# Dense layers of a long-convolution kernel: 25 tiles instead of 26, 22 of them 512 columns wide

## Chip, cores and metric

The kernel runs on one core of one Trainium2 chip. The metric is the device time of one execution in microseconds, as the median of several runs. Profiles are of one execution each; their times count from the first instruction of the span.

## What is computed

```
x, v: (1, 12480, 128)    pos_emb: (12480, 64)    w1: (64, 64)    w2: (64, 128)
h = relu(pos_emb @ w1) @ w2 * exp(-0.01 * pos)          # the filter, 12480 taps
y = irfft(rfft(x * v, 2S) * rfft(h, 2S))[:S]            # causal convolution along the sequence
a = x * y
a = relu(a @ moe_w_in) ** 2 @ moe_w_out                 # dense layer pair 1, width 2048
out = elu(a @ moe2_w_in) @ moe2_w_out                   # dense layer pair 2, width 2048
```

All of it is in fp32 in the reference; S = 12480, d_model = 128.

## The kernel before

The convolution is a two-factor Fourier transform of length 181 x 127 (`N1`, `N2`). A position is n1 * 127 + 63 + s * p: a row (p, s) holds the up to 99 positions (`R`) that share their distance p from the middle of a block of 127 and the side s. There are 127 rows, 98 or 99 positions each. Phase 1 folds and transforms the inputs over n1, phase 2 transforms over n2, multiplies by the filter's spectrum, transforms back over k2 and stores the result as `Zd` in DRAM. The last transform back, over k1, is done in phase 3, tile by tile, just ahead of the dense layers.

Columns here are positions. `SIZES` cuts the 127 rows into tiles: 4 rows, 24 times 5 rows, 3 rows. [...]

Phase 3 works on 26 tiles x 8 steps, written out as one sequence of steps `s`; the program order on each engine is the order in which this Python emits it (no scheduler moves it). For a tile and a step u, 256 of the 2048 hidden units are done:

- `mm1` multiplies the tile by a block of input weights, `mm2` adds the product with the output weights into the tile's y bank. Both use `mm6`: numbers and weights are split in a high and a low part, and six one-pass matmuls (type fp32r, 128 x 128 weights, the tile's columns as the moving operand) make up one product of two blocks (hi x hi, hi x lo, lo x hi). Each has a weight load of its own. A step has 24 such matmuls: 12 for `mm1` and `mm2` of the first layer pair (l = 0), 12 for those of the second (l = 1), which runs `LEAD` = 11 steps behind on an earlier tile.
- ScalarE and VectorE make the activations (L860, L864, L871 for pair 1; L795, L796, L852, L878 and a copy at L148 for pair 2). The low parts are subtractions at L145 (`sub`): on GpSimd for pair 1, on VectorE for pair 2 (`lo_of`).
- `fin` copies y out: to the second pair's input, or as `ys` to the output in DRAM.
- For the last tile (`t == NT - 1`) the second pair's `mm2` uses whole weights `wl` and plain fp32 matmuls (L751), two instead of six, each recorded as two.

Ahead of its first step a tile is loaded and prepared. `load(t)` issues eight transfers on SP's queue: five pieces of `Zd` into z, then the tile's transform tables ta and tb and its x. z, x, ta and tb have two buffers each, so a load waits for the preparation two tiles before it. It is emitted at step 0 of tile t - 2, tile 1's before the loop. `prep(t)` is a generator of which two pieces are emitted per step, from step 0 of tile t - 1 on (tile 1's from step 3 of tile 0): three operations on VectorE (L697), the transform back `ymm2` on TensorE (L619, L623, into a borrowed PSUM bank), the product with x on VectorE (L705), the rounding copy xh on ScalarE (L148) and the low part xl on VectorE (L145). xh and xl are what `mm1` reads. Tile 0's are made at the end of phase 2.

PSUM is full in phase 3: one double bank `h`, two double banks `h2`, two y banks. One bank holds 512 fp32 columns.

The output's columns, x and the tables stand in the order of the tiles' rows (`_perm`, `cols`).

Of the kernel before, what the change touches and what calls it, by code (L numbers as in the profile page):

```python
# [10 lines left out]
F32 = mybir.dt.float32  # L11
F32R = mybir.dt.float32r
U32 = mybir.dt.uint32
AF = mybir.ActivationFunctionType
ALU = mybir.AluOpType
# [4 lines left out]
S = 12480  # L20
D = 128
# [3 lines left out]
N2 = 127  # L25
CEN = N2 // 2
# [4 lines left out]
KA = K1 - 64  # L31
R = 99
SPLIT = S - (R - 1) * N2
SIZES = (4,) + 24 * (5,) + (3,)
KTAIL = K1 - 64
TBB = 6
WF = 5
# [19 lines left out]
def _tiles():  # L57
    seq = [(p, s) for p in range(CEN + 1) for s in (1, -1) if p or s == 1]
    out = []
    b = 0  # L60
    for g in SIZES:
        part = seq[b:b + g]
        right = [p for p, s in part if s == 1]
        left = [p for p, s in part if s == -1]
        if not out:
            part = [(p, 1) for p in right] + [(p, -1) for p in left]
        out.append((right, left, [R if s < 0 and CEN - p < SPLIT else R - 1 for p, s in part], part))
        b += g
    assert b == len(seq)
    return out  # L70


def tables():
    n1 = np.arange(R)
    k1 = np.arange(K1)
    k2 = np.arange(N2)
    pe, po = np.arange(CEN + 1), np.arange(1, CEN + 1)
    t = {}
    th = _angle(n1[:, None] * k1[None, :], N1)
    t["t1"] = np.stack([np.cos(th), -np.sin(th), -np.cos(th)], axis=2).reshape(R, 3 * K1)  # L80
    tf = np.zeros((2 * NP, N2, N2))
    k = k1[:, None, None] + N1 * k2[None, None, :]
    tf[:K1, :CEN + 1] = np.cos(_angle(pe[None, :, None] * k, L))
    tf[:K1, 0] = 0.5
    tf[:K1, CEN + 1:] = np.sin(_angle(po[None, :, None] * k, L))
    t["tf"] = np.zeros((NP, 128, 2 * N2))
    t["tf"][:, :N2] = tf.reshape(NP, 2, N2, N2).swapaxes(1, 2).reshape(NP, N2, 2 * N2)
    th = _angle(k2[:, None] * pe[None, :], N2)
    g = np.zeros((128, 128))
    g[:N2, 0] = 1.0  # L90
    g[:N2, 1:N2:2] = np.cos(th)[:, 1:]
    g[:N2, 2:N2:2] = np.sin(th)[:, 1:]
    t["g"] = g
    tl = _tiles()
    order = [s * p for p, s in tl[0][3]]
    at = _perm() - CEN
    c = np.where(k1 == 0, 1.0, 2.0)[:, None] / L
    th = _angle(k1[:, None] * at[None, :], L)
    re, im = c * np.cos(th), -c * np.sin(th)
    n = sum(tl[0][2])  # L100
    t["t3"] = np.stack([re[:, :n].reshape(K1, SIZES[0], -1), im[:, :n].reshape(K1, SIZES[0], -1)], axis=2)
    t["t3"] = t["t3"].reshape(K1, -1)
    t["ta"] = np.concatenate([re, im[:KA]])
    side = np.concatenate([np.full(nr, s) for _, _, nrs, rows in tl for (p, s), nr in zip(rows, nrs)])
    t["tb"] = np.concatenate([np.where(side == s, im[KA:], 0.0) for s in (1, -1)])
    sg = np.ones((128, 3))
    sg[:K1, 0] = sg[K1:, 1] = sg[K1 - KA:, 2] = -1.0
    t["sg"] = sg
    th = _angle((k[2 * PD:, 0, :, None, None] *
                 (np.array(order)[:, None] + N2 * n1[None, :R - 1])[None, None]), L).reshape(KD, N2, -1)  # L110
    t["t4"] = np.zeros((128, 2 * th[:, 0].size))
    t["t4"][:N2] = (2.0 / L * np.stack([np.cos(th), -np.sin(th)], axis=1)).transpose(2, 0, 1, 3).reshape(N2, -1)
    pos = _taps().astype(np.float32)
    ok = (pos >= 0) & (pos < S)
    win = np.where(ok, np.exp(np.float32(-0.01) * np.where(ok, pos, np.float32(0.0))), 0.0)
    win = win.transpose(2, 0, 1).reshape(R, 8, 2, 4, 2).transpose(0, 1, 2, 4, 3).reshape(R, 128)
    t["wz"] = np.concatenate([win, np.zeros((128 - R, 128))])
    return {k: np.ascontiguousarray(a, dtype=np.float32) for k, a in t.items()}
# [8 lines left out]
    return np.concatenate([a, np.zeros((1, a.shape[1]), a.dtype)])[np.where((at >= 0) & (at < S), at, S)]  # L127


def _perm():  # L130
    return np.concatenate([np.arange(nr) * N2 + CEN + s * p for _, _, nrs, rows in _tiles()
                           for (p, s), nr in zip(rows, nrs)])


class Build:
# [14 lines left out]
    def setup(self):  # L150
        nc = self.nc
        const = self.const = self.pool("const")
        self.dram = self.pool("dram", 1, DRAM)
        self.zero = const.tile([128, 128], F32, name="zero")
        nc.vector.memset(self.zero, 0.0)
        self.ebias = const.tile([128, 3], F32, name="ebias")
        self.sg = const.tile([128, 3], F32, name="sg")
        nc.vector.memset(self.ebias[:, 0:1], 1151.0)
        nc.vector.memset(self.ebias[:, 1:2], 255.0 * 8388608.0)
        self.Z = self.dram.tile([K1, 128, 2 * D], F32, name="Zd")  # L160
        self.wp = self.pool("wp")
        self.tiles = _tiles()
        self.st = {}

    def big(self, i, dt=F32):
# [439 lines left out]
    def cols(self, a, t):  # L605
        c = sum(sum(nrs) for _, _, nrs, _ in self.tiles[:t])
        return a[:, c:c + sum(self.tiles[t][2])]

    def ymm(self, ps, v, t3):
        for i in range(SIZES[0]):  # L610
            o = ps[i // 2][:, (R - 1) * (i % 2):(R - 1) * (i % 2 + 1)]
            for ri in range(2):
                self.nc.tensor.matmul(o, lhsT=v[:, i, ri, :], rhs=t3[:, i, ri], start=False, stop=(i % 2 == 1 and ri == 1))
# [24 lines left out]
    def phase3(self):  # L638
        nc, a = self.nc, self.a
        ctx0 = self.ctx  # L640
        with ExitStack() as self.ctx:
            gh = self.pool("gh3", 3)
            gp = self.pool("gp3", 2)
            xp = self.pool("xp3", 2)
            wk = self.pool("wk3", 1)
# [3 lines left out]
            psl = self.pool("psl", 2, PSUM)  # L649
            psy = self.pool("psy", 1, PSUM)  # L650
            tl = self.tiles
            NT = len(tl)
            xin = {}
            yps = {}
            lds = {}

            def width(t):
                n = sum(tl[t][2])
                return n, n + n % 2

            def load(t):
# [27 lines left out]
            def prep(t):  # L689
                right, left, nrs, rows = tl[t]  # L690
                n, ne = width(t)
                z, x, ta, tb, v, p0 = lds.pop(t)
                ka = K1 + KA
                for i, (side, k) in enumerate(((right, ka), (left, ka), (None, 128))):
                    q = slice(side[0] - p0, side[-1] - p0 + 1) if side else slice(0, v.shape[2])
                    zi = z[:k, i // 2, q]
                    nc.vector.scalar_tensor_tensor(out=v[:k, i, q], in0=zi[:, :, 1], scalar=self.sg[:k, i:i + 1],  # L697
                                                   in1=zi[:, :, 0], op0=ALU.mult, op1=ALU.add)
                    yield
                yield  # L700
                ps = aux()[:, 0]
                post.append(lambda: self.ymm2(ps, v, ta, tb, rows, nrs, p0))
                yield
                at = row(wk, "at")
                nc.vector.tensor_tensor(out=at[:, :n], in0=ps[:, :n], in1=x, op=ALU.mult)  # L705
                yield
                xh, xl = row(xp, "xh", F32R), row(xp, "xl", F32R)
                if ne > n:
                    nc.vector.tensor_copy(xh[:, n:ne], self.zero[:, 0:1])
                    nc.vector.tensor_copy(xl[:, n:ne], self.zero[:, 0:1])  # L710
                self.copy(xh[:, :n], at[:, :n])
                yield
                self.sub(nc.vector, xl[:, :n], at[:, :n], xh[:, :n].bitcast(F32))
                xin[t, 0] = (xh, xl)
                yield

            def mm1(t, l, u, odd=False):
# [39 lines left out]
            def fin(t, l):  # L757
                n, ne = width(t)
                y = yps[t, l]
                if l == 0:  # L760
                    xh, xl = row(xp, "xh1", F32R), row(xp, "xl1", F32R)
                    self.copy(xh[:, :ne], y[:, :ne])
                    yield
                    self.sub(nc.vector, xl[:, :ne], y[:, :ne], xh[:, :ne].bitcast(F32))
                    xin[t, 1] = (xh, xl)
                    return
                if t < NT - 3:
                    yield
                ys = row(ld, "ys")
                self.copy(ys[:, :n], y[:, :n])  # L770
                nc.sync.dma_start(out=self.cols(self.out, t), in_=ys[:, :n])

            seq = [(t, u) for t in range(NT) for u in range(8)]
            NS = len(seq)
# [25 lines left out]
                nc.gpsimd.tensor_tensor(out=wl[:, 2 * q:2 * q + 2], in0=w[:, :, 0], in1=w[:, :, 1], op=ALU.add)  # L800

            wl = wk.tile([128, NB, D], F32, tag="wl", name="wl")
            load(1)
            xin[0, 0] = self.x0
            one, two = {}, {}
            late = []
            LEAD = 8 + OFF
            for s in range(NS + LEAD + 2):
                k = s - LEAD
# [10 lines left out]
                if both:  # L820
                    t, u = seq[s]
                    if own is not None:
                        pair["s"] = own
                    if u == 0 and t + 2 < NT:
                        load(t + 2)
                    if u == (0 if t else 3) and t + 1 < NT:
                        bg.append(prep(t + 1))
                step()
                if both:
                    f = one[s] = {"t": t, "h": mm1(t, 0, u, k < 0 and (s == 1 or s > 0 and s % 2 == 0))}  # L830
# [102 lines left out]
```

## Time and profile before

| | |
|---|---|
| median of 3 runs | 1366.89 us (1365.93 to 1367.56) |
| the profiled execution's own time | 1366.67 us |
| its span, first to last instruction | 1364.9 us |
| TensorE busy | 99% of the span |
| VectorE, ScalarE, GpSimd busy | 87%, 82%, 45% |
| dense layers (phase 3) | from about 221 us to the end |

The profile's page gives busy time by engine, the chain of work that ended last (followed back from the last instruction, each step to what released it) and the costliest groups of instructions by source line. PE is TensorE, PEld its weight loads, DVE VectorE, ACT ScalarE, POOL GpSimd, SP the engine whose queue issues the transfers. Matmuls overlap their neighbours, so a single one's duration is longer than the spacing between two; the spacing is read from the pieces of the chain or from start times. A copy of y (`ys`) ends each tile of the second pair, so from one to the next is a tile's period.

### The profile page before, as it was taken

What the parts mean: (1) busy time and instruction counts of PE and PEld (TensorE: products, weight loads), DVE (VectorE), ACT (ScalarE), POOL (GpSimd) and SP (SyncE); (2) the same over time, 40 slices, a digit from 0 to 9 for tenths busy, and PEclk for the clock granted to TensorE, in tenths of its full rate; (3) what the DMA queues carried; (4) which work ended last, traced back from release to release, by engine and by line L of the source; (5) the groups of instructions that cost most, each with busy time, mean ns of one, the idle gap of its engine ahead of it and who ended that gap; (6) DMA issues with size and microseconds to landing.
All of it is one profiled execution on the core that took longest, in us unless ns stands there. A gap on an engine that the chain in (4) does not pass through costs nothing.

```text
span 1364.9 us, 19227 instructions
## 1 busy us (share of the span) xinstructions
PE 1351.7 (99%) x7150; PEld 1152.1 (84%) x7150; DVE 1183.9 (87%) x1234; ACT 1123.7 (82%) x1477; POOL 617.2 (45%) x342
## 2 busy tenths in 40 slices
PE   9999999999999999999999999999999999999998
PEld 9987667898888888888888888888888888888886
DVE  6759986789988989898988998898988898889897
ACT  6778775888888888888988888888888888888895
POOL 3039991445644444444444444444444444444432
PEclk9999999999999999999999999999999999999999
DMA  8746675201111011101110111101110111010000
GB/s 259 218 147 206 208 226 154 86 8 43 51 51 32 21 51 52 48 4 52 53 52 11 41 52 52 30 22 52 52 46 6 52 52 48 4 37 8 8 8 13
DMA packets 71483, 89.38 MB, mean 65 GB/s; under 512 B 5595, under 2 KB 65750, under 8 KB 71390
## 3 DMA queue, kind: packets, MB, share of 16 engines
q1 hardware_dynamic: 71246, 88.03, 21.6%
q8 instruction: 56, 0.92, 0.3%
q14 instruction: 37, 0.30, 0.1%
q10 hardware_dynamic: 144, 0.13, 0.1%
HBM read 69.78 MB, written 18.32 MB: 65 GB/s over the span
## 4 chain that ended last, share of the span: by engine, by line
PE 93%; POOL 2%; DVE 2%; issue 1%; ACT 1%; DMA 1%; SPq 0%; DVEq 0%; POOLq 0%; ACTq 0%
PE h L172 39%; PE y L172 38%; PE s L296 4%; PE u L482 2%; PE h L619 2%; PE v L505 2%; PE h L623 2%; PE h L354 1%; PE rt L341 1%; PE s L262 1%; POOL m L145 1%; POOL pt L497 1%; POOL pt L498 1%; PE y L751 0%; DMA xr<-in_post_dram 0%
## 5 line engine op out<-in xcount | busy, mean ns | idle before, releaser
L145 POOL TENSOR_TENSOR lo<-g,hi 128x980 fp32r<-128x980 f32 (+3 forms) x200 | 470.0, 2350 | 640.6 <-DVE tn L852 594.2
L172 PE MATMUL h<-xh,m 128*128 128x490 f32 (+4 forms) x1664 | 429.3, 380 | 1.8 <-ACT xh L148 1.1
L172 PE MATMUL y<-hi,m 128*128 128x490 f32 (+4 forms) x1632 | 426.0, 383 | 0.0
L172 PEld LDWEIGHTS h<-xh,m 128*128 128x128 f32 x1664 | 312.4, 189 | 52.4 <-DVE g L864 1.9
L172 PEld LDWEIGHTS y<-hi,m 128*128 128x128 f32 x1632 | 303.5, 189 | 50.5 <-ACT ys L148 4.2
L795 ACT ACTIVATE tn<-h 128x980 f32<-128x980 f32 (+4 forms) x208 | 202.9, 975 | 161.4 <-PE h L172 155.8
L852 DVE SCALAR_TENSOR_TENSOR tn<-ex,tn 128x980 f32<-128x980 f32 (+4 forms) x208 | 241.9, 1163 | 107.6 <-ACT ex L796 105.4
L145 DVE TENSOR_TENSOR lo<-ex,hi 128x980 fp32r<-128x980 f32 (+4 forms) x200 | 251.2, 1256 | 0.0
L864 DVE SCALAR_TENSOR_TENSOR g<-h,r 128x980 f32<-128x980 f32 (+4 forms) x208 | 239.6, 1152 | 9.7 <-ACT r L860 9.3
L172 PE MATMUL y<-lo,m 128*128 128x490 f32 (+4 forms) x816 | 245.8, 382 | 1.9 <-POOL lo L145 1.5
L172 PE MATMUL h<-xl,m 128*128 128x490 f32 (+4 forms) x832 | 247.3, 378 | 0.0
L878 DVE SCALAR_TENSOR_TENSOR ex<-tn,h 128x980 f32<-128x980 f32 (+4 forms) x208 | 238.4, 1146 | 1.4
L871 ACT ACTIVATE hi<-r 128x980 fp32r<-128x980 f32 (+4 forms) x208 | 211.9, 1019 | 0.5
L860 ACT ACTIVATE r<-h 128x980 f32<-128x980 f32 (+4 forms) x208 | 204.2, 982 | 6.7 <-PE h L172 4.6
L148 ACT ACTIVATE hi<-ex 128x980 fp32r<-128x980 f32 (+3 forms) x200 | 206.4, 1032 | 0.0
L796 ACT ACTIVATE ex<-h 128x980 f32<-128x980 f32 (+4 forms) x208 | 201.0, 966 | 0.0
L172 PEld LDWEIGHTS y<-lo,m 128*128 128x128 f32 x816 | 153.7, 189 | 30.1 <-POOL lo L145 3.6
L172 PEld LDWEIGHTS h<-xl,m 128*128 128x128 f32 x832 | 156.4, 189 | 24.6
L497 POOL TENSOR_TENSOR pt<-pt 127x256 f32<-127x256 f32 x43 | 37.3, 867 | 69.6 <-DVE pt L494 69.1
L505 PE MATMUL v<-pt,g 127*128 127x512 f32 (+1 forms) x92 | 48.7, 615 | 2.3 <-DVE pt L494 2.3
L494 DVE TENSOR_TENSOR pt<-u,hh 127x512 f32<-127x512 f32 (+1 forms) x46 | 31.1, 676 | 19.9 <-PE u L482 19.2
L697 DVE SCALAR_TENSOR_TENSOR v<-z,sg 118x256 f32<-118x256 f32 (+3 forms) x75 | 43.0, 573 | 0.0
(85 smaller groups left out, 1050.4 us busy)
## 6 DMA issues: line engine op xcount, KB each, us to landing
Zd<-z SPq DMA_DIRECT2D x45, 256.0 KB
z<-Zd SPq DMA_DIRECT2D x48, 192.0 KB
z<-Zd SPq DMA_DIRECT2D x48, 136.5 KB
xc<-in_xv_dram SPq DMA_DIRECT2D x16, 392.0 KB
tb<-in_tf_dram SPq DMA_DIRECT2D x46, 127.0 KB
raw<-in_moe_w_in_dram SPq DMA_DIRECT2D x8, 512.0 KB
raw<-in_moe_w_out_dram SPq DMA_DIRECT2D x8, 512.0 KB
m<-in_xv_dram SPq DMA_DIRECT2D x8, 392.0 KB
```

The source lines that it names most:

```text
L145: return eng.tensor_tensor(out=out, in0=a, in1=b, op=ALU.subtract)
L148: self.nc.scalar.activation(out=out, in_=in_, func=AF.Copy)
L172: self.nc.tensor.matmul(outs[b], lhsT=w[:, b, h], rhs=x[b], start=first and i in ((0,) if one else (0, 2)), stop=last and i in ((5,) if on ...
L296: nc.tensor.matmul(pv[b:e, j // 2, :, j % 2], lhsT=fb[j][q], rhs=self.t1[:, :, q:q + 2], start=(j % 2 == 0), stop=(j % 2 == 1))
L505: nc.tensor.matmul(v, lhsT=self.g[:N2], rhs=pt.rearrange("p j r d -> p (j r d)"), start=True, stop=True)
L795: nc.scalar.activation(out=e["tn"], in_=e["h"], func=AF.Tanh, scale=0.5)
L796: nc.scalar.activation(out=e["ex"], in_=e["h"], func=AF.Exp)
L852: after = nc.vector.scalar_tensor_tensor(out=pa["em"], in0=pa["ex"], scalar=1.0, in1=pa["tn"], op0=ALU.add, op1=ALU.mult)
L860: nc.scalar.activation(out=f["r"], in_=f["h"], func=AF.Relu)
L864: nc.vector.scalar_tensor_tensor(out=f["g"], in0=f["h"], scalar=0.0, in1=f["r"], op0=ALU.max, op1=ALU.mult)
L871: nc.scalar.activation(out=f["hi"], in_=f["r"], func=AF.Square)
L878: nc.vector.scalar_tensor_tensor(out=pa["g"], in0=pa["em"], scalar=0.0, in1=pa["h"], op0=ALU.min, op1=ALU.max)
```

## The change

The 127 rows are cut as 4, 23 times 5, 3, and 5. The last five rows (493 columns) are no tile of the dense layers any more. They are loaded, transformed back, multiplied by x and split once, in tile 1, into two buffers that stay (`rest`: rh, rl). The dense layers then run over `NT` = 25 tiles. Tiles 0 and 1 stay at 392 and 490 columns. Each of tiles 2 to 23 copies the next columns of the kept group behind its own until it has 512 (22 columns, 20 or 19), and the last tile, of 295 columns, takes the 39 that are left, which makes 334. The two copies per tile are on GpSimd, at the end of the tile's preparation. The order of the output's columns follows (`_perm`, `outs`), while x and the tables keep the order of the rows.

The loads and preparations get tables of places: the kept group's load stands where tile 2's was (step 0 of tile 0), tile 2's at step 6 of tile 0, tile 3's at step 3 of tile 1; from tile 4 on it is as before. The kept group is prepared from step 0 of tile 1, tile 2 from step 3 of tile 1, and from tile 3 on it is as before. Steps fall from 208 to 200.

```diff
-SIZES = (4,) + 24 * (5,) + (3,)
+SIZES = (4,) + 23 * (5,) + (3, 5)
+NT = len(SIZES) - 1
+FULL = 512
+FILL = 2
...
+def _fill():
+    tl = _tiles()
+    left = sum(tl[NT][2])
+    out, b = [], 0
+    for t in range(NT):
+        n = 0 if t < FILL else min(FULL - sum(tl[t][2]), left - b)
+        out.append((b, b + n))
+        b += n
+    assert b == left
     return out
...
+    def outs(self, t):
+        n = [sum(self.tiles[i][2]) + self.fill[i][1] - self.fill[i][0] for i in range(t + 1)]
+        return self.out[:, sum(n[:t]):sum(n)]
...
             def width(t):
-                n = sum(tl[t][2])
+                b, e = self.fill[t] if t < NT else (0, 0)
+                n = sum(tl[t][2]) + e - b
                 return n, n + n % 2
...
             def prep(t):
...
-                nc.vector.tensor_tensor(out=at[:, :n], in0=ps[:, :n], in1=x, op=ALU.mult)
+                nc.vector.tensor_tensor(out=at[:, :r], in0=ps[:, :r], in1=x, op=ALU.mult)
                 yield
-                xh, xl = row(xp, "xh", F32R), row(xp, "xl", F32R)
+                xh, xl = (row(xp, "xh", F32R), row(xp, "xl", F32R)) if t < NT else rest
...
-                self.copy(xh[:, :n], at[:, :n])
+                self.copy(xh[:, :r], at[:, :r])
                 yield
-                self.sub(nc.vector, xl[:, :n], at[:, :n], xh[:, :n].bitcast(F32))
-                xin[t, 0] = (xh, xl)
+                self.sub(nc.vector, xl[:, :r], at[:, :r], xh[:, :r].bitcast(F32))
+                if t < NT:
+                    b, e = self.fill[t]
+                    if e > b:
+                        for o, i in zip((xh, xl), rest):
+                            nc.gpsimd.tensor_copy(o[:, r:n], i[:, b:e])
+                    xin[t, 0] = (xh, xl)
                 yield
...
-                nc.sync.dma_start(out=self.cols(self.out, t), in_=ys[:, :n])
+                nc.sync.dma_start(out=self.outs(t), in_=ys[:, :n])
...
+            rest = [wk.tile([128, 512], F32R, tag=nm, name=nm) for nm in ("rh", "rl")]
...
+            loads = {(0, 0): NT, (0, 6): 2, (1, 3): 3, **{(t, 0): t + 2 for t in range(2, NT - 2)}}
+            preps = {(0, 3): 1, (1, 0): NT, (1, 3): 2, **{(t, 0): t + 1 for t in range(2, NT - 1)}}
...
-                    if u == 0 and t + 2 < NT:
-                        load(t + 2)
-                    if u == (0 if t else 3) and t + 1 < NT:
-                        bg.append(prep(t + 1))
+                    if (t, u) in loads:
+                        load(loads[t, u])
+                    if (t, u) in preps:
+                        bg.append(prep(preps[t, u]))
```

## Rows read from the trace of the kernel before

**Rows 1.** The page's first part: busy time, share of the span, instructions.

```profile
PE 1351.7 (99%) x7150; PEld 1152.1 (84%) x7150; DVE 1183.9 (87%) x1234; ACT 1123.7 (82%) x1477; POOL 617.2 (45%) x342
```

**Rows 2.** The page's fourth part: the chain that ended last, by engine.

```profile
PE 93%; POOL 2%; DVE 2%; issue 1%; ACT 1%; DMA 1%; SPq 0%; DVEq 0%; POOLq 0%; ACTq 0%
```

**Rows 3.** Busy time by windows: one tile of 490, then a pair 492 and 493.

```profile
core 0: us, PE busy (x) PEld busy (x) DVE busy (x) ACT busy (x) POOL busy (x), PEclk, DMA share, GB/s
659.05:703.35 44.30, 44.30 (x209) 38.66 (x208) 39.41 (x38) 37.96 (x44) 18.98 (x8) 1.00 0.14 40
926.20:1015.60 89.40, 89.40 (x418) 75.94 (x417) 79.61 (x78) 76.31 (x87) 38.29 (x16) 1.00 0.14 40
```

**Rows 4.** Waits of PE and PEld, 305 to 1283: total, times, longest (us).

```profile
PEld y L172 <- ACT ys L148: 4.0, 21, 0.2
```

**Rows 5.** The chain's pieces in a tile of 490: start, length (us), what.

```profile
632.80 2.64 PE h L172 x12
635.44 0.20 PE h L619 x2
...
637.09 0.36 PE h L623 x2
637.45 2.64 PE y L172 x12
```

**Rows 6.** The chain's pieces where tiles of 492 and 493 alternate.

```profile
957.22 2.66 PE h L172 x12
959.88 2.68 PE y L172 x12
```

**Rows 7.** The chain's pieces in tile 0 (392) and at tile 1's start.

```profile
236.32 1.07 PE h L172 x6
237.39 1.06 PE y L172 x6
...
240.59 1.33 PE h L172 x6
```

**Rows 8.** The chain's pieces in the last tile (296 columns).

```profile
1351.30 0.81 PE h L172 x6
1352.11 1.00 PE y L751 x4
```

**Rows 9.** Timeline of TensorE in phase 2: plain fp32 matmuls of 512 columns.

```profile
181.07 1.02 PE L505 MATMUL v<-pt,g 127*128 127x512 f32 x2
181.93 1.03 PE L482 MATMUL u<-xt,tb 127*127 127x256 f32 x4
```

**Rows 10.** Groups by line and shape: count, busy us, mean ns, idle before.

```profile
L852 DVE SCALAR_TENSOR_TENSOR tn<-ex,tn 128x980 f32<-128x980 f32 x88 | 104.1, 1182 | 46.1 <-ACT ex L796 45.2
...
L852 DVE SCALAR_TENSOR_TENSOR tn<-ex,tn 128x592 f32<-128x592 f32 x8 | 6.2, 774 | 1.7 <-ACT ex L796 1.6
...
L795 ACT ACTIVATE tn<-h 128x980 f32<-128x980 f32 x88 | 87.3, 992 | 69.7 <-PE h L172 69.7
...
L795 ACT ACTIVATE tn<-h 128x592 f32<-128x592 f32 x8 | 5.3, 664 | 5.4 <-PE h L172 5.3
...
L145 POOL TENSOR_TENSOR lo<-g,hi 128x980 fp32r<-128x980 f32 x88 | 209.7, 2384 | 286.2 <-DVE tn L852 239.9 <-DVE g L864 35.1 <-PE y L172 11.2
...
L145 POOL TENSOR_TENSOR lo<-g,hi 128x592 fp32r<-128x592 f32 x8 | 11.8, 1473 | 23.0 <-DVE tn L852 23.0
```

**Rows 11.** Timeline of VectorE and GpSimd in one tile: start, length, idle before.

```profile
640.24 1.18 DVE L145 TENSOR_TENSOR lo<-ex,hi 128x980 fp32r<-128x980 f32 x1
...
644.46 0.66 DVE L145 TENSOR_TENSOR xl<-at,xh 128x490 fp32r<-128x490 f32 x1
...
655.24 2.33 POOL L145 TENSOR_TENSOR lo<-g,hi 128x980 fp32r<-128x980 f32 x1 [2.96 <-DVE tn L852]
...
657.18 1.42 DVE L145 TENSOR_TENSOR lo<-ex,hi 128x980 fp32r<-128x980 f32 x1
...
660.52 2.33 POOL L145 TENSOR_TENSOR lo<-g,hi 128x980 fp32r<-128x980 f32 x1 [2.95 <-DVE tn L852]
```

**Rows 12.** Timeline of SP: first and last transfers of the third tile load.

```profile
234.45 1.04 SPq L667 DMA_DIRECT2D z<-Zd  x2
...
244.22 0.38 SPq L675 DMA_DIRECT2D x<-in_xt_dram  x1
```

More of the change, by code (lines that the diff above doesn't have):

```diff
@@ L70, in _tiles @@
     return out
+def _fill():
[7 more added lines that the diff above has]
+    assert b == left
+    return out
 def tables():
@@ L95, in tables @@
     order = [s * p for p, s in tl[0][3]]
-    at = _perm() - CEN
+    at = np.concatenate(_rows()) - CEN
     c = np.where(k1 == 0, 1.0, 2.0)[:, None] / L
@@ L127, in _take, with _rows @@
     return np.concatenate([a, np.zeros((1, a.shape[1]), a.dtype)])[np.where((at >= 0) & (at < S), at, S)]
+def _rows():
+    return [np.concatenate([np.arange(nr) * N2 + CEN + s * p for (p, s), nr in zip(rows, nrs)])
+            for _, _, nrs, rows in _tiles()]
 def _perm():
-    return np.concatenate([np.arange(nr) * N2 + CEN + s * p for _, _, nrs, rows in _tiles()
-                           for (p, s), nr in zip(rows, nrs)])
+    at = _rows()
+    return np.concatenate([np.concatenate([at[t], at[NT][b:e]]) for t, (b, e) in enumerate(_fill())])
 class Build:
@@ L162, in setup @@
         self.tiles = _tiles()
+        self.fill = _fill()
         self.st = {}
@@ L651, in phase3 @@
             tl = self.tiles
-            NT = len(tl)
             xin = {}
@@ L691, in prep @@
                 n, ne = width(t)
+                r = sum(nrs)
                 z, x, ta, tb, v, p0 = lds.pop(t)
@@ L910 @@
     arrays = {
-        "xt": np.ascontiguousarray(x.reshape(S, D)[perm].T), "xv": xv, "post": post, "w2": w2,
+        "xt": np.ascontiguousarray(x.reshape(S, D)[np.concatenate(_rows())].T), "xv": xv, "post": post, "w2": w2,
     }
```

## The prediction

> **What bounds the kernel now.** Read the page's first part, then its chain of waits, then the windows. TensorE is busy for 99% of the span [rows 1], at the full granted clock of 1.00 [rows 3], and 93% of the chain that ended last is TensorE [rows 2]. So the end moves only if the sum of TensorE's matmul spacings moves, or if some other engine starts to hold TensorE up. The reader is to see in the windows that the other engines have room: in one tile of 490 columns (44.30 us) VectorE is busy 39.41, ScalarE 37.96 and GpSimd 18.98 us [rows 3]. In the whole steady stretch the only wait on TensorE's side is 0.2 us for ScalarE's copy of y, 21 times, 4.0 us in all [rows 4].
>
> The pieces of the chain give what one matmul costs in the stream, which the mean durations on the page don't, since neighbours overlap. Spacing = length of a piece divided by its matmuls. A piece of 12 takes 2.64 us at 490 columns, 220.0 ns each [rows 5], 2.66 at 492 (221.7 ns) and 2.68 at 494 (223.3 ns) [rows 6]. Narrow tiles: 392 columns take 1.06 to 1.07 us for six, 177.5 ns [rows 7]; 296 take 0.81 us for six, 135 ns [rows 8].
>
> What a spacing holds beyond N/2.4 ns (one column per period of the 2.4 GHz that the granted clock 1.00 [rows 3] stands for) is 11.7 ns at 296, 14.2 at 392, 15.8 at 490, 16.7 at 492, 17.5 at 494. It is not constant: it grows with the width. That decides this change.
>
> **What the change removes.** The column count stays: 12480 of output, of which six padding columns go (six tiles of 493 ran as 494). A dense tile is eight steps of 24 matmuls, 192 in all, and one whole tile goes: 26 tiles become 25. But the columns of that tile come back in the others, 22 more in each tile of 490, 19 or 20 in the rest. So the gain is 192 matmuls times that part of the spacing which does not depend on the width, and nothing else of size.
>
> Slope from 392 to 490: (220.0 - 177.5)/98 = 0.434 ns per column; from 296 to 490: 85/194 = 0.438. Both extrapolate 22 columns to 512 at 220.0 + 9.5 or 9.6; I take 229.5 ns. The fixed part is then 220.0 - 490 x 0.434 = 7.3 ns. No one-pass matmul of 512 columns stands in this trace, so both ends are needed. Low end: the least excess of any row, 11.7 ns at 296, on 512/2.4 = 213.3: 225.0 ns. Lower still are the full-precision matmuls of 512 columns, two in 0.86 us [rows 9], 430 ns each, twice 215, so two passes over the columns with 1.7 ns beyond 213.3 in each. They do twice the streaming behind each weight load, and I use them only as a sign that full width has no penalty by itself. High end: the excess rose 1.7 ns over the last four columns, and if it reaches 19.2 at 512 the spacing is 232.5 ns. (Carrying the full local slope, 0.83 ns per column from 490 to 494, to 512 would give 238; nothing between 296 and 490 supports that over 18 columns.) I take the line, 229.5, because 490 is the widest spacing that is the same in every piece, and 392 and 296 lie on a line with it.
>
> Sum against the profiled execution (span 1364.9, time 1366.67, which is 1.8 around the span; the median of the runs is 1366.89, 0.2 above it):
> - Before, 24 tiles of five rows: 11 x 44.30 [rows 3] = 487.3, and 13 of 492 and 493, a pair of which takes 89.40 [rows 3], 6.5 x 89.40 = 581.1. Sum 1068.4.
> - After: one of 490, 44.30; 22 of 512, each 44.30 + 192 x 9.5 ns = 46.12, so 1014.6; and the back transform of the five shared rows, which has no tile of its own any more: one such transform runs from 635.44 to 637.45 in a tile of before, 2.0 us [rows 5]. Sum 1060.9. That is 7.5 less.
> - The last tile grows from 296 to 334 columns (295 of its own, 39 taken). It has 144 one-pass matmuls, 38 x 0.434 = 16.5 ns each, 2.4 us; and 32 two-pass ones of the second layer, now 1.00 us for four [rows 8], 250 ns each or two passes, 2 x 38/2.4 = 32 ns each, 1.0 us. With 0.2 us for the elementwise work behind the last matmul, plus 3.6.
> - Net 3.9 us less: span 1361.0, time 1362.8.
>
> Every nanosecond of the spacing at 512 is worth 22 x 192 = 4224 ns, 4.2 us. The break-even spacing is 229.5 + 3.9/4.2 = 230.4 ns. So the whole question lies within the two ends.
>
> At the Trainium skill's page "TensorE: Matmul & The Clock Gate", section "Back-to-back issue gap", a warm isolated matmul of N columns is followed after N/2.4 + 2.5 ns. This trace does not agree in the size: at 490 that gives 206.7 ns where the row has 220.0. If its 2.5 ns were the only fixed part, dropping 192 matmuls would be worth 0.5 us by it and six padding columns another 0.5, which speaks against the change; that outcome is the first rival below.
>
> **What it adds and moves, at nothing.** 46 copies of 19 to 39 columns on GpSimd, two a tile. GpSimd takes 1473 ns for 592 elements and 2384 for 980 [rows 10], 2.35 ns per element, so about 0.05 us of work each plus a start, an estimate of 0.2 us. They stand behind the low part of the first layer's product in GpSimd's queue, and behind them stands the next one, which waits about 3 us for VectorE in every step anyway [rows 11]. They come right behind VectorE's last subtraction of the preparation, which in the tile of [rows 5] starts at 644.46 [rows 11]; the back transform before it stands in the tile's third step, so the next tile begins five steps of 5.28 us after that step's end, near 669. That is over 20 us of cover. The cover gone, each would cost at most its 0.4 us, 22 times, 9 us. VectorE loses the padding copies of the tiles of 493, off the path: nothing.
>
> The elementwise work grows with the columns too. VectorE: 774 ns at 592, 1182 at 980, 1.05 ns per element, so 46 ns on each of 32 instructions of a tile, 1.5 us: 40.9 busy of 46.1, the share of before (89%). ScalarE: 664 to 992, 0.85 ns, 37 ns on 40: 39.5 of 46.1, 86% as before [rows 3, 10]. No engine comes nearer to being the bound.
>
> Moved: the shared group is loaded where tile 2 was, tile 2's eight transfers go behind it in SP's queue to step 6 of tile 0, tile 3's to step 3 of tile 1. In the trace of before the third load is what stands in that place: its first transfer issues at 234.45, its last at 244.22, because it waits for the buffers of the first [rows 12]. Tile 2's preparation now starts three steps after tile 1's first matmul (240.59 [rows 7]), near 250, which leaves 6 us of cover. Without the cover, up to 6 us once. Tile 1 has two preparations instead of one; in its first three steps the second layer is not yet running, so VectorE has room. Outputs: the same bytes, one transfer fewer.
>
> **The rivals.**
> 1. *No fixed part: nothing gained.* Spacing grows in proportion, 220.0 x 512/490 = 229.9 ns, or along a line through 296 and 494, 230.8. Time 1362.8 + 0.4 x 4.2 = 1364.5 up to 1368.3; call it 1366.5. For it: the excess grows with the width with every wider row of [rows 5 to 8]. Against it: a strict proportion would put 296 at 132.9, the row has 135.
> 2. *The excess climbs (slower).* From 490 to 494 it gained 1.7 ns in four columns. In this rival the widest operand meets a limit that narrower ones don't; at 232.5 ns the time is 1362.8 + 3.0 x 4.2 = 1375.5. It decides from 230.4 + 2.7/4.2 = 231.0 ns on. Against it: 492 and 494 may only be awkward widths.
> 3. *The excess falls back.* 490, 492 and 494 are no round widths; 512 fills the tile row. With the 11.7 ns of the 296 row the spacing is 225.0 and the time 1362.8 - 4.5 x 4.2 = 1343.8. For it: the jump between 490 and 494 shows that the excess isn't smooth, and the full-width two-pass matmuls have next to none [rows 9]. Against: 296 and 392 are round in eights and lie on the line.
> 4. *A wait takes the place.* The copies, or a VectorE that they hold up, make TensorE wait about 0.5 us per tile: 22 x 0.5, time 1374. VectorE's subtraction already takes 1.42 us beside GpSimd's where it takes 1.18 alone [rows 11]. The skill's page "SBUF — State Buffer", section "Who interferes with whom", has such pairs block each other when both read SBUF with two inputs on VectorE; the trace agrees by that 0.24 us. Against: 5 us of VectorE's idle time in each tile [rows 3].
>
> **How the numbers follow.** Forecast (line): 0.37. Rival 1: 0.22. Rival 2: 0.15. Rival 3: 0.19. Rival 4: 0.07. 0.2% is 2.7 us, about what a measurement of this kernel tells from no change: faster means below 1364.2, slower above 1369.6. The forecast's own spread of half a nanosecond either way is 1360.7 to 1364.9, so 0.06 of its 0.37 lies within 0.2%. Faster: 0.31 + 0.19 = 0.50. Same: 0.06 + 0.22 = 0.28. Slower: 0.15 + 0.07 = 0.22. The range reaches to the centres of rivals 3 and 2, 1344 to 1376, which leaves out about half of each, 0.17. The forecast alone: 1359 to 1367.
>
> **What would show it.** In the chain, pieces of 12 matmuls of 512 columns: 2.754 us is the forecast, 2.70 or less rival 3, 2.79 or more rival 2. Tile periods between two copies of y: 46.1 us. No new wait on TensorE's side in the table of waits; if GpSimd or VectorE appears there some 20 times, rival 4. The back transform of the shared rows: one more block of 2.0 us inside tile 1. The prediction is wrong if the spacing at 512 isn't within half a nanosecond of 229.5, and by 4.2 us for each nanosecond.

## The result, and the profile after

The changed kernel takes 1354.55 us (median of 4 runs, 1353.99 to 1355.37) against 1366.41 for the kernel before (4 runs, 1365.67 to 1367.56). The ratio is 0.9913, 95% interval 0.9896 to 0.9930: faster by 0.87%, 11.9 us. The forecast was 3.9 us, with a range of 1344 to 1376. The profiled execution took 1353.99 us, its span is 1352.2, 12.7 less than before.

The page's first and fourth parts of the changed kernel, to be held against [rows 1, 2]:

```profile
PE 1337.2 (99%) x6958; PEld 1114.2 (82%) x6958; DVE 1180.1 (87%) x1191; ACT 1119.6 (83%) x1435; POOL 644.9 (48%) x380
...
PE 91%; DVE 3%; POOL 2%; issue 1%; DMA 1%; ACT 1%; SPq 0%; DVEq 0%; POOLq 0%; ACTq 0%
```

There are 192 matmuls fewer, one tile, and TensorE is still the chain. VectorE's share of the chain went from 2% to 3%. The place of most of that is found below: at the one wait shown there the chain turns to VectorE and follows it back for some 20 us, while the wait itself is 1.7 us.

Busy time by windows in the changed kernel, two tiles of 512 columns (columns as in [rows 3]):

```profile
core 0: us, PE busy (x) PEld busy (x) DVE busy (x) ACT busy (x) POOL busy (x), PEclk, DMA share, GB/s
672.83:718.49 45.66, 45.66 (x209) 37.98 (x208) 41.03 (x38) 39.47 (x44) 21.05 (x10) 1.00 0.13 39
1129.46:1175.12 45.66, 45.66 (x209) 37.98 (x208) 41.02 (x38) 39.47 (x44) 21.05 (x10) 1.00 0.13 39
```

A tile's period is 45.66 us; the forecast was 46.12, and the tile of 490 took 44.30 [rows 3]. VectorE has 41.0 us of work in it and ScalarE 39.5, as forecast (40.9 and 39.5).

The chain's pieces in one of these tiles, to be held against [rows 5]:

```profile
626.68 2.81 PE y L193 x12
...
645.82 2.72 PE h L193 x12
648.53 0.20 PE h L644 x2
...
650.18 0.36 PE h L648 x2
650.54 2.75 PE y L193 x12
653.29 2.72 PE h L193 x12
656.01 2.72 PE y L193 x12
```

Twelve matmuls of 512 columns take 2.72 us, 226.7 ns each. Two pieces of a tile are longer: the one right behind the back transform (2.75) and the one in which a copy of y ends a tile (2.81). The forecast was 2.754 (229.5 ns). At 4.2 us per nanosecond these 2.8 ns would be 12 us; the period, which also holds these two, is 0.46 us below the forecast, 10.1 us in 22 tiles. The back transform takes 2.01 us, from 648.53 to 650.54, as before.

The waits of TensorE's matmuls and of its weight loads in the changed kernel from 240 to 1260 us, all of them (total, times, longest):

```profile
PE h L193 <- DVE g L898: 1.7, 1, 1.7
...
PEld y L193 <- ACT ys L168: 4.4, 20, 0.2
PEld h L193 <- DVE g L898: 2.5, 3, 2.0
```

The wait of 0.2 us for the copy of y is that of [rows 4]. The one for VectorE's g is new. It comes once, in tile 1 (the weight load's 2.0 us are the same wait). The timeline of the changed kernel at that place (start, length, engine, line):

```profile
250.08 0.61 DVE L723 SCALAR_TENSOR_TENSOR v<-z,sg 118x384 f32<-118x384 f32 x1
250.21 2.65 POOL L165 TENSOR_TENSOR lo<-g,hi 128x980 fp32r<-128x980 f32 x1 [1.43 <-DVE g L898]
...
250.60 2.78 DVE L165 TENSOR_TENSOR rl<-at,rh 128x493 fp32r<-128x493 f32 x1
...
253.31 0.47 DVE L723 SCALAR_TENSOR_TENSOR v<-z,sg 118x256 f32<-118x256 f32 x1
...
253.70 1.17 DVE L898 SCALAR_TENSOR_TENSOR g<-h,r 128x980 f32<-128x980 f32 x1
...
254.92 0.49 PE L193 MATMUL h<-xh,m 128*128 128x490 f32 x1 [1.65 <-DVE g L898]
```

The kept group's low part (rl) stands on VectorE behind the first operation of tile 2's preparation (L723 at 250.08). GpSimd's subtraction began at 250.21 and ends at 252.86, so rl begins beside it; it lasts 2.78 us, to 253.38, where such a subtraction takes 0.66 [rows 11]. Behind it stands the activation g (L898), and for that TensorE waits.

### The profile page after: what moved, and what is told of

It reads as the page before. It is cut to its first block, busy times and chain, and to the rows that moved or that the text cites. A ratio compares the mean times of both kernels' runs of the same rounds, so it can differ in the third digit from the quotient of the medians.

```text
span 1352.2 us, 18781 instructions
## 1 busy us (share of the span) xinstructions
PE 1337.2 (99%) x6958; PEld 1114.2 (82%) x6958; DVE 1180.1 (87%) x1191; ACT 1119.6 (83%) x1435; POOL 644.9 (48%) x380
## 4 chain that ended last, share of the span: by engine, by line
PE 91%; DVE 3%; POOL 2%; issue 1%; DMA 1%; ACT 1%; SPq 0%; DVEq 0%; POOLq 0%; ACTq 0%
PE h L193 38%; PE y L193 38%; PE s L317 4%; PE u L503 2%; PE v L526 2%; PE h L644 2%; PE h L648 2%; PE h L375 1%; PE rt L362 1%; PE s L283 1%; DVE g L898 1%; DVE lo L165 1%; POOL m L165 1%; POOL pt L518 1%; POOL pt L519 1%
## 5 line engine op out<-in xcount | busy, mean ns | idle before, releaser
L165 POOL TENSOR_TENSOR lo<-g,hi 128x1024 fp32r<-128x1024 f32 (+2 forms) x192 | 467.6, 2436 | 598.2 <-DVE tn L886 496.0
L193 PE MATMUL h<-xh,m 128*128 128x512 f32 (+3 forms) x1600 | 421.3, 385 | 3.4 <-DVE g L898 2.3
L193 PE MATMUL y<-hi,m 128*128 128x512 f32 (+2 forms) x1568 | 418.9, 389 | 0.0
L886 DVE SCALAR_TENSOR_TENSOR tn<-ex,tn 128x1024 f32<-128x1024 f32 (+3 forms) x200 | 240.4, 1202 | 99.8 <-ACT ex L827 98.7
L165 DVE TENSOR_TENSOR lo<-ex,hi 128x1024 fp32r<-128x1024 f32 (+3 forms) x192 | 248.5, 1294 | 0.0
L898 DVE SCALAR_TENSOR_TENSOR g<-h,r 128x1024 f32<-128x1024 f32 (+3 forms) x200 | 238.4, 1192 | 9.2 <-ACT r L894 9.2
L193 PE MATMUL y<-lo,m 128*128 128x512 f32 (+2 forms) x784 | 240.4, 387 | 2.1 <-POOL lo L165 1.7
L193 PE MATMUL h<-xl,m 128*128 128x512 f32 (+3 forms) x800 | 242.1, 384 | 0.0
L912 DVE SCALAR_TENSOR_TENSOR ex<-tn,h 128x1024 f32<-128x1024 f32 (+3 forms) x200 | 237.1, 1185 | 1.4
L905 ACT ACTIVATE hi<-r 128x1024 fp32r<-128x1024 f32 (+3 forms) x200 | 209.8, 1049 | 0.5
L723 DVE SCALAR_TENSOR_TENSOR v<-z,sg 118x384 f32<-118x384 f32 (+3 forms) x75 | 43.0, 573 | 0.0
```

Source lines behind the costliest of these rows:

```text
L165: return eng.tensor_tensor(out=out, in0=a, in1=b, op=ALU.subtract)
L193: self.nc.tensor.matmul(outs[b], lhsT=w[:, b, h], rhs=x[b], start=first and i in ((0,) if one else (0, 2)), stop=last and i in ((5,) if on ...
L886: after = nc.vector.scalar_tensor_tensor(out=pa["em"], in0=pa["ex"], scalar=1.0, in1=pa["tn"], op0=ALU.add, op1=ALU.mult)
L898: nc.vector.scalar_tensor_tensor(out=f["g"], in0=f["h"], scalar=0.0, in1=f["r"], op0=ALU.max, op1=ALU.mult)
L905: nc.scalar.activation(out=f["hi"], in_=f["r"], func=AF.Square)
L912: nc.vector.scalar_tensor_tensor(out=pa["g"], in0=pa["em"], scalar=0.0, in1=pa["h"], op0=ALU.min, op1=ALU.max)
```

## The experiments

Their chain pieces and windows are read as above. Where a kernel has a trace and no ratio, it was run once.

**1. The width without the change.** All 26 tiles kept, the columns of the five-row tiles filled up with zeros to 512 (the copy into xl is changed in the same way):

```diff
             def width(t):
                 n = sum(tl[t][2])
-                return n, n + n % 2
+                return n, 512 if 0 < t < NT - 1 else n + n % 2
...
-                    nc.vector.tensor_copy(xh[:, n:ne], self.zero[:, 0:1])
+                    nc.vector.tensor_copy(xh[:, n:ne], self.zero[:, :ne - n])
...
```

> The kernel before, its 26 tiles kept, with all 24 five-row tiles padded with zero columns to 512 (no column is shared, the output is the same). It prices the width alone. If 512 columns cost 226.7 ns a matmul, as the changed kernel's chain shows, a tile's period is 45.6 to 45.7 us against 44.30 (490) and 44.70 (492 and 493): 11 x 1.3 + 13 x 0.95 = 27 us more, about 1393. The line of the prediction (229.5 ns) would give 11 x 1.82 + 13 x 1.4 = 38 us more, about 1405. If the gain of the change were in the fewer tiles and not in the width, the period here would be that of the line.

Measured: 1394.02 us, ratio 1.0196 (1.0181 to 1.0212), 27 us more. Pieces of its chain:

```profile
651.20 2.72 PE h L172 x12
653.92 2.72 PE y L172 x12
```

So 226.7 ns belongs to the width of 512, with or without shared columns. The gain is the rest: the 24 wide tiles here carry zeros worth about one tile, and the changed kernel, which has real columns in their place and one tile less, takes 39.5 us less than this one.

**2. Which widths are cheap.** The same kernel with other paddings, three tiles each, run once:

```diff
-                return n, n + n % 2
+                return n, 496 + 2 * ((t - 1) // 3) if 0 < t < NT - 1 else n + n % 2
```

> The kernel before with tiles 1 to 24 padded with zero columns in threes to 496, 498, 500, 502, 504, 506, 508 and 510. One trace then holds the spacing at each. Theory multiples of 16: a width that is a multiple of 16 costs N/2.4 + 13.3 ns, and the widths behind it cost more until the next one: 496 costs 220.0 ns like 490, and 498 to 510 lie at 223 to 230, above 512's 226.7 at some point. Rival line (0.434 ns per column): 496 costs 222.6, 504 226.1, 510 228.7, each step of two columns 0.87. Rival full bank: all of these lie on the line and only 512 falls below it.

Measured: 1389.8 us. Pieces of its chain at 498, 502, 504, 508 and 510 columns, each inside a stretch in which all matmuls have that width:

```profile
471.04 2.72 PE y L172 x12
...
742.25 2.68 PE y L172 x12
...
878.25 2.72 PE y L172 x12
...
1154.79 2.74 PE h L172 x12
...
1285.68 2.72 PE h L172 x12
```

None of the three held. 496 costs 2.68 (223.3 ns), not 220.0; no width lies above 2.74 away from the back transforms; and from 504 to 512 nothing rises, but for 508, whose pieces go from 2.72 to 2.74.

**3. Narrower widths.** The kernel before with `SIZES = 13 * (4,) + 15 * (5,)`, the padding copies of experiment 1, and

```diff
-                return n, n + n % 2
+                return n, (400, 416, 432, 464, 496, 512, 512, 512, 512)[(t - 1) // 3] if 0 < t < NT - 1 else n + n % 2
```

> The kernel before cut into 13 tiles of four rows and 15 of five, the four-row tiles 1 to 12 padded with zero columns in threes to 400, 416, 432, 464, the five-row ones to 496 and then 512. It has 28 tiles and is slower for that; its spacings count, not its time. Theory multiples of 16 (N/2.4 + 13.3): 180.0, 186.7, 193.3, 206.7, 220.0, 226.7 ns. Rival line (0.434 N + 7.3): 180.9, 187.8, 194.8, 208.7, 222.6, 229.5 ns. Rival full bank: the line for all but 512.

Measured: 1420.37 us. Its pieces at 400, 416, 464 and 496 columns:

```profile
301.60 2.16 PE h L172 x12
...
430.77 2.26 PE y L172 x12
...
668.91 2.52 PE y L172 x12
...
802.45 2.68 PE h L172 x12
```

That is 180.0, 188.3, 210.0 and 223.3 ns. The rule for multiples of 16 fails from 416 on, by 1.7 to 3.3 ns; the line is closer there, but 464 and 496 lie 1.3 and 0.7 ns off it, and 512, at 226.7 here too, 2.8.

**4. Steps.** After this the suspicion was a staircase. The same cut into tiles, with other widths, the five-row tiles unpadded:

```diff
-                return n, n + n % 2
+                return n, 468 + 6 * ((t - 1) // 3) if 0 < t < 13 else n + n % 2
```

> The kernel before cut into 13 tiles of four rows and 15 of five, the four-row tiles 1 to 12 padded with zero columns in threes to 468, 474, 480 and 486, the five-row ones unpadded; 28 tiles, so its spacings count and not its time. The widths from 498 to 512 cost the same within 0.6 ns (226.7 to 227.3), but for 500 and 502 at 224. Theory steps: the spacing rises in steps of about 6.7 ns with flat pieces between them, and 490 stands at the end of one as 512 does; 480 and 486 then cost 219 to 220 like 490, and 468 or 474 about 213 to 215. Rival: below 496 the spacing is a smooth line, 468 211.0, 474 213.4, 480 215.8, 486 218.3 (from 464 at 209.5 to 490 at 220.0), and only the stretch up to 512 is flat.

Measured: 1458.85 us. Pieces at 468, 474, 480 and 486 columns:

```profile
327.75 2.54 PE y L172 x12
...
455.21 2.56 PE y L172 x12
...
586.71 2.60 PE h L172 x12
...
717.92 2.64 PE h L172 x12
```

486 costs the same as 490, as the steps said; 480 does not, it stands 3.3 ns below. So there are steps, half as high as expected.

All widths together, as the length of a piece of twelve in microseconds, in units of 0.04 (3.33 ns a matmul), and by the prediction's line, 12 x (0.434 N + 7.3) ns:

| columns | piece of 12 | units | line |
|---|---|---|---|
| 400 | 2.16 | 54 | 2.17 |
| 416 | 2.26 | 56.5 | 2.25 |
| 432 | 2.35 | 58.75 | 2.34 |
| 464 | 2.52 | 63 | 2.50 |
| 468 | 2.54 | 63.5 | 2.52 |
| 474 | 2.56 | 64 | 2.56 |
| 480 | 2.60 | 65 | 2.59 |
| 486, 490 | 2.64 | 66 | 2.62, 2.64 |
| 492 | 2.64 or 2.67 | 66 or 66.75 | 2.65 |
| 494, 496 | 2.68 | 67 | 2.66, 2.67 |
| 498 | 2.72 | 68 | 2.68 |
| 500, 502 | 2.68 | 67 | 2.69, 2.70 |
| 504, 506, 510 | 2.72 | 68 | 2.71 to 2.74 |
| 512 | 2.72 | 68 | 2.75 |

The row of 492 is from the kernel before. The piece of 2.66 us in [rows 6], which the prediction read as 492, holds six matmuls of 492 columns and six of 494, the width at which a tile of 493 runs:

```profile
957.94 0.60 PE L172 MATMUL h<-xl,m 128*128 128x492 f32 x2
958.38 1.05 PE L172 MATMUL h<-xh,m 128*128 128x494 f32 x4
```

Where all twelve have 492, the pieces are of two kinds:

```profile
909.74 2.67 PE y L172 x12
...
1088.65 2.64 PE y L172 x12
```

From 474 on the lengths sit on whole units, but for one kind at 492 and for some pieces at 508. Since 492 has two lengths, the width alone doesn't set the spacing. One unit is the time of eight columns at 2.4 GHz. 490 to 512 are 22 columns and only two units apart.

**5. Is the top flat in the kernel's time too?** The changed kernel with

```diff
-FULL = 512
+FULL = 506
```

> The changed kernel with 506 instead of 512 as the full width: 22 tiles give up 6 columns each, 132 in all, and the last tile takes them (466 instead of 334 columns). Theory (the spacing is flat from 504 to 512, 2.72 us for 12): the 22 tiles keep their period of 45.66 us, and the last tile costs 144 x 132 x 0.434 ns + 32 x 132 x 2/2.4 ns = 8.3 + 3.5 = 11.8 us more: 1366, as slow as the kernel before. Rival (a line of 0.434 ns per column): the 22 tiles get 22 x 192 x 6 x 0.434 ns = 11.0 us shorter and the time is 1355.3.

Measured: 1365.44 us, ratio 0.9987 (0.9977 to 0.9996), 10.9 us more than the changed kernel's 1354.55. A piece of its chain, and the last tile's (466 columns):

```profile
699.84 2.72 PE h L193 x12
...
1350.86 1.29 PE h L193 x6
1352.15 1.56 PE y L782 x4
```

The line would have had 1355.3. The 22 tiles keep their pieces of 2.72 us, and their period between two copies of y is 45.60 us instead of 45.66: the last six columns of each tile are as good as free, and the last tile, where they go otherwise, pays the full price for them. The change has its gain from these columns: with 506 nearly all of it is gone.

**6. The wait in tile 1.** Tile 2's preparation one step later:

```diff
-            preps = {(0, 3): 1, (1, 0): NT, (1, 3): 2,
+            preps = {(0, 3): 1, (1, 0): NT, (1, 4): 2,
```

> The changed kernel with tile 2's preparation one step later (step 4 of tile 1 instead of 3), so that the kept group's last subtraction on VectorE no longer stands behind the first operation of tile 2's preparation. Theory: in the changed kernel that subtraction came late, ran beside GpSimd's and took 2.78 us, which held up the activation behind it and TensorE for 1.65 us; moved, it takes about 0.7 and the first copy of y comes 1.5 to 1.8 us earlier (306.4 instead of 308.08), span near 1350.5. Rival: the two preparations in tile 1 simply need VectorE's time, and the same wait comes a step later; span 1352.

Measured: 1355.57 us, ratio 0.9913 (0.9897 to 0.9930), no gain over the changed kernel. VectorE's timeline has the subtraction at its usual length:

```profile
251.40 0.66 DVE L165 TENSOR_TENSOR rl<-at,rh 128x493 fp32r<-128x493 f32 x1
```

but TensorE's waits from 215 to 310 us have a new one, for tile 2's first copy on GpSimd:

```profile
PE h L193 <- POOL xh L744: 1.5, 1, 1.5
```

The cause of the wait was read rightly, and the remedy lost as much: tile 2's preparation now ended so late that its first copy, behind a subtraction in GpSimd's queue, was not done when the tile began. From the first dense matmul to the first copy of y it is 88.0 us, in the changed kernel 87.4.

**7. The two preparations swapped.** Tile 2 back at its old place, the kept group behind it, sharing from tile 3 on; the changed kernel again beside it on the same chip.

```diff
-FILL = 2
+FILL = 3
...
-            loads = {(0, 0): NT, (0, 6): 2, (1, 3): 3, **{(t, 0): t + 2 for t in range(2, NT - 2)}}
-            preps = {(0, 3): 1, (1, 0): NT, (1, 3): 2, **{(t, 0): t + 1 for t in range(2, NT - 1)}}
+            loads = {(0, 0): 2, (0, 6): NT, (1, 4): 3, **{(t, 0): t + 2 for t in range(2, NT - 2)}}
+            preps = {(0, 3): 1, (1, 0): 2, (1, 4): NT, **{(t, 0): t + 1 for t in range(2, NT - 1)}}
```

> The changed kernel with the kept group loaded after tile 2 and prepared behind it (step 4 of tile 1), tile 2 at the place it had in the kernel before, and the sharing begun at tile 3: tile 2 stays at 490 columns and the last tile takes 356 instead of 334. Theory (the 1.7 us lost in tile 1 come from the order of the two preparations, and the kept group then has over a tile until its first use): no wait of 1 us or more on TensorE's side after 240 us, first copy of y about 1.5 us earlier than in the changed kernel counted from the first dense matmul (86.0 instead of 87.4); the narrower tile 2 gives 1.3 us and the 22 columns in the last tile cost 2.0; in all about 1 us less, near 1353.6. Rival (two preparations in tile 1 cost TensorE time wherever they stand): the wait stays, and the time is 0.7 us more than the changed kernel's.

> The changed kernel as it is, beside the one with the two preparations swapped, on the same chip: 1354.5.

Measured: 1353.39 us (ratio 0.9903, 0.9887 to 0.9920) against 1354.18 (0.9908, 0.9893 to 0.9923). The times alone don't tell 0.8 us apart. The trace does: TensorE's waits from 240 to 1300 us are

```profile
PE h L193 <- DVE g L898: 0.3, 1, 0.3
```

and the first copy of y comes 85.9 us after the first dense matmul (87.6 in the other), as expected (86.0); about 0.2 us of that is the narrower tile 2 (an estimate, 36 matmuls at 6.7 ns). From the first dense matmul to the last copy of y it is 1127.2 us, in the other 1128.6. The two preparations fit into tile 1 in this order, with 0.3 us of waiting.

**8. The copies.** Each of the 46 copies three times:

```diff
-                        for o, i in zip((xh, xl), rest):
+                        for o, i in 3 * list(zip((xh, xl), rest)):
```

> The changed kernel with each of the 46 copies from the kept group done three times into the same place. Theory (the copies are hidden: GpSimd is idle for 24 us of a tile's 45.66, and the first matmul that reads them comes over 20 us later): no wait of TensorE on GpSimd in the steady stretch, period 45.66, time 1354.5 within 1 us. Rival (the copies, or VectorE held up by them, cost the path something): 92 copies more at 0.2 to 1.2 us, of which some part appears as waits, 2 us or more.

Measured: 1355.38 us, ratio 0.9919 (0.9902 to 0.9935), 0.8 us above the changed kernel. Its windows, in a tile:

```profile
672.83:718.49 45.66, 45.66 (x210) 37.96 (x209) 41.16 (x39) 39.44 (x44) 22.60 (x15) 1.00 0.13 39
```

The period is the same, and no wait of TensorE on GpSimd appears from 240 to 1260 us. The profiled execution is 1.6 us longer than the changed kernel's, and 1.1 of that is a later start of the dense layers (first matmul at 221.78 instead of 220.65), before any copy. From there to the last copy of y it is 1128.8 us; the two traces of the changed kernel (the first one and that of experiment 7) have 1128.3 and 1128.6. The copies are hidden.

## Why the prediction was right about the direction and a third of the size

- **The forecast's place.** 1354.55 lies in the range of 1344 to 1376, but outside the forecast's own 1359 to 1367, a little nearer to the forecast (1362.8) than to rival 3 (1343.8). By its own sign, a spacing within half a nanosecond of 229.5, the prediction was wrong on that term, by 2.8 ns. The line stood only 0.9 ns from break-even (230.4); the same error the other way would have made the kernel slower. That the change is faster was given 0.50, and that the error fell on the good side is luck.
- **TensorE's spacings set the end: right.** The sum below closes with them, the transform and one wait, and no other engine became the bound: VectorE is busy for 90% of a tile's period, 89% before.
- **The spacing at 512 columns: the term that was mis-sized.** The prediction carried a slope of 0.434 ns per column over 22 columns, 9.5 ns. Measured are 6.7 ns in the pieces (experiments 1 to 5), and 7.1 on the mean of a tile (45.66 less 44.30 us over 192 matmuls). 22 tiles at 45.66 instead of 46.12 us are 10.1 us. The line was drawn through 296, 392 and 490; it is right within 1.4 ns from 400 to 480 columns, but from 474 on the spacing moves in steps of 3.33 ns, and 512, at the far end of its step, stands two of them above 490, where the line has nearly three. The jump between 490 and 494 in [rows 5, 6], which the prediction set aside as awkward widths, was one such step, 3.3 ns; its 221.7 ns at 492 (an excess of 16.7) is a mixture, and 492 alone has 220.0 or 222.5. Rival 3 had the direction (the excess falls back to 13.3 ns beyond N/2.4, from 15.8 at 490) and the opposite error, 225.0. Rival 2 fell: the steep piece from 490 to 498 ends there. In rival 1 the line through 296 and 494 gives 231.4 ns at 512, not 230.8, and so 1370.8 us instead of 1368.3; the forecast doesn't rest on it.
- **The formula of the Trainium skill** ("TensorE: Matmul & The Clock Gate", section "Back-to-back issue gap") is given there for an isolated matmul and has 215.8 ns at 512. This trace, a stream of one-pass matmuls with a weight load each, has 226.7. The rival that went with it (nothing gained) fell.
- **The last tile: right.** Forecast 3.4 us for 38 columns, 0.089 us per column. Experiment 5 gives 132 columns more: its last copy of y stands at 1361.14 us against 1348.98, 12.16 later. Of this 1.23 us are a later start of its dense layers, and 22 periods of 45.60 us hide 1.4 us more: 12.3 us, 0.093 per column. For 38 columns this makes 3.5.
- **The back transform of the kept group, 2.0 us: right.** In the changed kernel it runs in tile 1 from 246.07 to 247.94 us, 1.9 us (the two rows below are its start and the first matmul behind it). From the first dense matmul to the first copy of y it is 87.4 us, 83.7 before: this transform, the wait of 1.7 us, and about 0.2 us for tile 2's greater width.

```profile
246.07 0.36 PE L644 MATMUL h<-ta,v 118*128 118x99 f32 x2
...
247.94 1.18 PE L193 MATMUL y<-hi,m 128*128 128x490 f32 x4
```

- **The move, costed at nothing: wrong by 1.7 us.** The transfers had the cover that was counted (tile 2's last x issues at 244 and its preparation starts at 250). What failed is "VectorE has room": there was room, but rl stood at a moment when GpSimd subtracts. The prediction had seen the mechanism (rival 4: 1.42 us for 1.18) and priced it for the copies in the steady stretch, where it costs nothing, not for the subtraction in tile 1, where 0.66 us became 2.78. By the Trainium skill's page "SBUF — State Buffer", section "Who interferes with whom", VectorE with two inputs in SBUF contends with GpSimd's reads for a shared pair of ports, and one of the two blocks the other wholly; the trace agrees here, rl ends 0.5 us after GpSimd's operation. Experiment 7 takes nearly all of the cost away.
- **The copies hidden: right** (experiment 8), with the limit that experiment 6 shows: where a tile's preparation ends too late, TensorE waits for them. Rival 4 fell: no wait of TensorE comes some 20 times.

The sum: 3.9 us less was forecast, the spacing takes off another 10.1, and the wait adds 1.7. That is 12.3 us less, and the span fell by 12.7, of which 0.3 us are an earlier start of the dense layers.

What stays open: why the spacing moves in steps of 3.33 ns, why 498 stands a step above 500 and 502, why 492 has two spacings in one kernel, and why the excess over N/2.4 at 512 (13.3 ns) lies below the 15.8 to 17.5 ns of 474 to 496. The runs show the steps, not their cause. What bears on them besides the width, as the two spacings at 492 show that something does, wasn't tested, and most of the padded widths were run in one execution alone. The version of experiment 7 is shorter than the changed kernel by its trace; by its time it isn't told apart.

## What to carry to other kernels

Where a stream of equal matmuls is the bound, measure the spacing at the width that is meant to be used before extrapolating from others: padding the existing tiles with zero columns gives it in one run, without building the change. Filling tiles to the full 512 columns paid here because the last six columns of each tile cost next to nothing, while the same columns in the narrower last tile cost their full price (experiment 5). When a change moves work, look at what then runs beside it on the other engine, and not only at whether the engine has time left: VectorE's subtraction with both inputs in SBUF took four times as long beside GpSimd's.

## What was not expected of the hardware

- The spacing of one-pass matmuls with a weight load each, at the granted clock of 1.00, sits on multiples of 3.33 ns (averaged over twelve) for the widths from 474 to 512 that were measured, but for one kind of piece at 492 (222.5 ns, the other kind 220.0) and some at 508; single widths are out of order (498: 226.7 ns, 502: 223.3 ns).
- A copy of 19 columns on GpSimd took 0.19 us, but 1.24 when it began beside VectorE's subtraction. The timeline of the changed kernel shows both kinds, one behind the other:

```profile
934.63 1.22 DVE L165 TENSOR_TENSOR lo<-ex,hi 128x1024 fp32r<-128x1024 f32 x1
934.66 1.24 POOL L744 CAST xh<-rh 128x19 fp32r<-128x19 f32 x1
935.84 0.19 POOL L744 CAST xl<-rl 128x19 fp32r<-128x19 f32 x1
```
